# Stacked weights moved to low addresses, raw w2 rows above them, stack and bias preparation moved to earlier steps

## The chip, the cores and the metric

The kernel runs on one core of one Trainium2 chip. The metric is the device time of one execution in microseconds. The core has five engines that run in parallel, each in its own program order: PE (TensorE, matmuls; PEld is its weight load), DVE (VectorE), ACT (ScalarE), POOL (GpSimd) and SP (SyncE, which here only issues DMA transfers). SBUF is the on-chip memory; a tile there has 128 partitions, and an address below is the byte offset in each partition. PSUM takes the results of matmuls, in banks.

## The reference

A linear attention block gated by a feed-forward block, S = 2048 rows, D = 576, H = 32 heads of 18, F = 4608:

```python
xn = layernorm(A_x)
q, k, v = split(xn @ A_wqkv)                 # 32 heads
pq, pk = phi(q), phi(k)                      # phi(t) = where(t > 0, t + 1, exp(t)) + 1e-6
kv, z = sum_s pk * v, sum_s pk               # state of each head
s = ((pq @ kv) / (pq @ z + 1e-6)) @ A_wo
h = gelu(xn @ B_w1 + B_b1)                   # 2048 x 4608
g = silu(h @ B_w2 + B_b2)
return A_x + s * g
```

All is float32. The kernel keeps the accuracy by splitting each operand into a high part, which is the value rounded to PE's own format (`hi`, a copy on ACT), and a low part, the remainder (`lo`, a subtraction on DVE), and multiplies high by high, high by low and low by high.

## The kernel before, in words

The attention part comes first and ends near 281 us of the span. The feed-forward part follows: 18 chunks, two halves of the rows (`half`) times nine groups of 512 hidden columns (`c`). A chunk computes the hidden values of its group for 1024 rows and adds their product with `w2` to the accumulator `macc`. Both products use a scheme with seven block products in place of eight (`UP` and `ORDER` list them), for which sums of blocks are formed beforehand.

A chunk is laid out in 28 steps, `base` to `base + 27`. Steps 0 to 13 are the up-projection: two pairs, seven block products each, of seven matmuls with 512 columns (`Up`). The first six of the seven take `w1` operands over 128 rows of the inner dimension. The seventh, `self.w.rest(i)`, takes the *stacked weights*: D = 576 is four times 128 and a rest of 64, and the rests of a product's operands are stacked into one 128-row operand. Steps 14 to 27 are the down-projection: seven block products twice, of twelve matmuls with 288 columns (`product`). After every step `at_step` emits what the table `plans` holds for it, in the order in which `add` put it there: splits, sums, loads and stores for this chunk and the next. In this part the instructions of DVE, ACT, POOL and PE keep exactly the order in which they are emitted (`in_order`); each engine does its work in that order and waits where the next piece is not ready. SP is not in that list: the framework's scheduler orders its DMA issues, mostly as emitted.

Stacked weights. The seven rests of a pair lie in two tiles (`W1.load_rest`): two in a part of the tile `low`, in the region of the normalized input (byte 74016 to 84256 of a partition), and five in `we`, from the pool `xe` at the upper end of SBUF (187360 to 192480, two buffers). Products 1 and 2 use the former, products 3 to 7 the latter. The pool `xe` also holds `mid`, five slices of 512 columns: three for the up-projection's partial sums, `mid[:, 3]` for the temporary of product 7 of the hidden operands (`HOps.S`, steps 7 and 13, read until step 15) and `mid[:, 4]` for a `w1` temporary.

Stacks. `Rest` and `Rest2` build the stacks themselves: load four raw rows, split the first three (`hi` 0, `lo` 0, `store` 0 to DRAM), form four sums in place (`sums`), split those (`hi` 1, `lo` 1, `store` 1). Four of them are made inside the feed-forward part, in the first halves' chunks c = 2, 3, 5 and 6 (`REST_CHUNK`, `plan_rest2`). They borrow tiles of the hidden operands: the raw rows `h4h`, the first group `h1h` and `h1l`, the second group `h3h` and `h3l`. The same chunk needs `h3h` at step 12 for the high part of hidden operand 2 of the second pair (`HBUF`).

Raw `w2` rows. A chunk of the first half splits its `w2` operands from a raw tile of 1152 KB (`load_w2_raw`, pool `w2rp`, one buffer, 107808 to 117024). The one for chunk 0 is loaded during the last round of the attention part, after the raw `w1` tiles of pairs 0 and 1, in the region whose order is kept on all engines.

Bias. `load_bias` loads two halves of `b2` into one row group of `macc`, in the first half from SP before chunk 0, in the second half from POOL at step 5 of chunk 9, after the finished values there have been stored to `c_dram`. `set_bias` copies them on ACT to the rest of the four accumulators of a chunk with c = 0, at steps 10, 11, 13 and 14.

The last chunk (`plain`) and the gating end the kernel.

Of the kernel before, what the change touches and what calls it, by code (L numbers as in the profile page):

```python
# [15 lines left out]
P = 128  # L16
# [29 lines left out]
def linear_attention_gated_ffn(ctx, tc, x, wqkv, wo, w1, w1e, b1, w2, b2, out):  # L46
# [820 lines left out]
    w1p = ctx.enter_context(tc.tile_pool(name="w1p", bufs=2, reuse_waits="tile"))  # L867
    w2rp = ctx.enter_context(tc.tile_pool(name="w2rp", bufs=1, reuse_waits="tile"))

    def load_w2_raw(n):  # L870
        raw = w2rp.tile([P, 2, 2, CF // 2, HD], F32, tag="w2raw", name=f"w2raw{n}")
        nc.sync.dma_start(raw.rearrange("p r n a d -> p (r n a d)"), w2[n % NC])
        return raw
# [158 lines left out]
    class W1:  # L1032
# [49 lines left out]
        def load_rest(self):  # L1082
            n = self.n % NP
            a = xe.tile([P, 5, P], F32R, tag="we", name=f"we{self.n}", bufs=2)
            b = low[:, 16 + 2 * (n % 2) :][:, :2]
            nc.sync.dma_start(b.bitcast(F32), we_dram[n // 4][:, n % 4, :2])
            nc.sync.dma_start(a.bitcast(F32), we_dram[n // 4][:, n % 4, 2:])
            self.re = a, b
# [33 lines left out]
    kept = []  # L1122
    w1t, w2_raw0 = {}, []

# [4 lines left out]
    for r in range(NPAIR + 2):  # L1129
# [63 lines left out]
        if 1 <= r < NPAIR:  # L1193
# [10 lines left out]
            if r == 7:  # L1204
                w1t[0], w1t[1] = W1(0), W1(1)
                w2_raw0.append(load_w2_raw(0))
        if r == 0:
# [36 lines left out]
    pse.close()  # L1244
    ph2.close()
    right.close()
    psum = ctx.enter_context(tc.tile_pool(name="psum", bufs=3, space=PSUM, reuse_waits="tile"))
# [10 lines left out]
    load_x_extra(0)  # L1258
    mid = xe.tile([P, 5, 512], F32, name="mid")
    w1t[0].load_rest()  # L1260
    for d, t in kept:
        nc.sync.dma_start(d, t)
# [84 lines left out]
    class Rest2(Rest):  # L1347

        def raw(self):
            return self.tile("h4h").bitcast(F32)  # L1350

# [8 lines left out]
    def plan_rest2(base, key):  # L1360
        def load():
            rests[key] = Rest2(*key)

        add(base - 4, load)
        for at, what, *args in (
            (2, "hi", 0), (3, "lo", 0), (3, "store", 0), (3, "sums", DV), (5, "hi", 1), (6, "lo", 1), (6, "store", 1),
        ):
            add(base + at, lambda what=what, args=args: getattr(rests[key], what)(*args))

    class W2:  # L1370
# [5 lines left out]
        def load_raw(self):  # L1376
            self.raw = raw = load_w2_raw(self.n) if self.n else w2_raw0[0]
            self.B = lambda r, n: raw[:, r, n]
# [285 lines left out]
    for step in range(n_chunks):  # L1664
# [4 lines left out]
        if c == 0:  # L1669
            if half:  # L1670
                add(base + 5, load_bias, nc.gpsimd)
            for at, m in zip((10, 11, 13, 14), (C11, C21, C22, C12)):
                add(base + at, set_bias, m)
# [150 lines left out]
```

## Time and profile before

| | |
|---|---|
| median of 3 runs | 1116.15 us (1115.54 to 1118.18) |
| the profiled execution | 1114.53 us, its span 1112.8 us |
| mean granted TensorE clock | 0.997 |
| PE busy | 1091.2 us, 98% of the span |
| DVE, ACT, POOL busy | 822.9, 515.6, 459.6 us |
| DMA moved | 295.02 MB, mean 265 GB/s |

How to read the rows that follow. A row of a timeline gives the start and the duration in us, the engine, the line of the kernel, the operation, what is written and what is read (out<-in), the shapes and the number of instructions merged; in brackets stands how long the engine was idle before it and what ended that. SPq marks an issue on SP's queue, whose duration is that of the issue alone. A row of the waits gives who waited for whom, the total in us, how often, and the longest. A row of a group gives busy us and mean ns after the first bar and the idle time before it after the second. A row of a window gives its bounds, its length, the busy time and number of instructions of PE, PEld, DVE, ACT and POOL, the granted clock, the DMA share and GB/s. A matmul's duration is longer than the distance between two matmuls, since they are pipelined and their ends are modelled. Numbers in names such as `w__4785` tell one `w2` operand from another.

### The profile page before, as it was taken

To read this page: it belongs to the slowest core of one execution; us is meant where nothing else is said; L and a number is where in the kernel's file an instruction comes from. 1 tells how busy PE (TensorE), PEld (TensorE's weight loads), DVE (VectorE), ACT (ScalarE), POOL (GpSimd) and SP (SyncE) were. 2 spreads that over 40 slices of the span, in tenths; PEclk is the share of its full clock that TensorE was granted. 3 is DMA by queue.
4 is the path that set the end of the run, shared out by engine and by line. 5 is a ranking of instruction groups with operands and counts; after the bars stand their busy time and mean duration, and the time that the engine had idled before them with its cause. 6 is when DMAs were issued, how large, how long until landed. Compare 5 with 4: busy or idle time off the path is not lost.

```text
span 1112.8 us, 19015 instructions
## 1 busy us (share of the span) xinstructions
PE 1091.2 (98%) x6888; PEld 1008.3 (91%) x6888; DVE 822.9 (74%) x1284; ACT 515.6 (46%) x945; POOL 459.6 (41%) x423
## 2 busy tenths in 40 slices
PE   8999999999999999999999999999999999999998
PEld 8999999999798888889888899898898998989987
DVE  6777567996698888888888888676485674764876
ACT  7776565554645544455443544524233242242342
POOL 6855534665445254453443514324234143242310
PEclk9999999999999999999999999999999999999999
DMA  5999828887988889788896979997767677767342
GB/s 196 310 292 341 301 82 261 316 336 264 369 295 309 294 275 370 238 315 296 277 370 223 326 221 350 385 339 266 247 221 226 198 237 227 230 216 227 93 149 113
DMA packets 121051, 295.02 MB, mean 265 GB/s; under 512 B 12797, under 2 KB 36605, under 8 KB 118911
## 3 DMA queue, kind: packets, MB, share of 16 engines
q1 hardware_dynamic: 115391, 282.32, 71.7%
q0 software_dynamic: 4992, 10.32, 5.4%
q8 instruction: 54, 0.88, 0.3%
q10 hardware_dynamic: 576, 1.18, 0.3%
q14 instruction: 38, 0.31, 0.1%
HBM read 180.39 MB, written 108.66 MB: 260 GB/s over the span
## 4 chain that ended last, share of the span: by engine, by line
PE 85%; DMA 5%; DVE 5%; ACT 3%; issue 2%; POOL 1%; SPq 0%; DVEq 0%; POOLq 0%; ACTq 0%
PE pm L1468 33%; PE a L1306 8%; PE zy L1306 8%; PE e L1306 8%; PE ps_s L997 5%; PE b L1306 5%; PE pl L477 5%; PE e L421 3%; PE a L421 2%; PE z L421 2%; PE pd L1583 2%; PE ps_kva L530 1%; DMA c_dram<-macc 1%; DVE h_l L1030 1%; PE b L421 1%
## 5 line engine op out<-in xcount | busy, mean ns | idle before, releaser
L1027 ACT CAST h_h<-g 128x512 fp32r<-128x512 f32 x204 | 120.1, 621 | 148.9 <-PE pm L1468 138.3
L1030 DVE TENSOR_TENSOR h_l<-g,h_h 128x512 fp32r<-128x512 f32 x204 | 168.9, 828 | 13.3 <-ACT g L1314 3.1
L1476 DVE TENSOR_TENSOR macc<-macc,pm 128x576 f32<-128x576 f32 x136 | 102.2, 751 | 39.2 <-PE pm L1468 39.1
L1306 PE MATMUL a<-xH,wa 128*128 128x512 f32 x288 | 101.0, 391 | 0.0
L1478 DVE TENSOR_TENSOR macc<-pm,macc 128x576 f32<-128x576 f32 x98 | 73.7, 756 | 20.4 <-PE pm L1468 19.2
L1314 ACT ACTIVATE g<-b,b1c 128x512 f32<-128x512 f32 x36 | 24.8, 690 | 132.2 <-DVE b L1332 132.2
L1436 POOL TENSOR_TENSOR mid<-g 128x512 f32<-128x512 f32 x34 | 46.8, 1375 | 92.1 <-ACT g L1314 92.1
L1323 ACT COPY mid<-a 128x512 f32<-128x512 f32 x36 | 21.2, 588 | 94.6 <-PE a L1306 94.6
L1306 PEld LDWEIGHTS a<-xH,wa 128*128 128x128 f32 x288 | 54.1, 188 | 11.1
L1430 POOL TENSOR_TENSOR g<-g 128x512 f32<-128x512 f32 x34 | 50.2, 1477 | 22.4 <-DVE h_l L1030 20.8
L1326 DVE TENSOR_TENSOR mid<-b,mid 128x512 f32<-128x512 f32 x36 | 24.7, 685 | 44.7 <-PE b L1306 42.7
L1433 POOL TENSOR_TENSOR g<-g 128x512 f32<-128x512 f32 x34 | 52.3, 1538 | 11.3 <-DVE h_l L1030 9.7
L1306 PE MATMUL a<-xL,wa 128*128 128x512 f32 x144 | 56.6, 393 | 0.0
L1554 POOL TENSOR_TENSOR fin1l<-fin1h,fin1l 128x288 f32<-128x288 f32 x8 | 6.5, 808 | 119.3 <-DMA fin1l<-s_dram 85.4
L1306 PE MATMUL e<-xSH,wb 128*128 128x512 f32 x144 | 50.6, 392 | 0.5 <-DVE b L1332 0.5
L1306 PE MATMUL zy<-xSH,w 128*128 128x512 f32 x144 | 50.3, 390 | 0.0
L1306 PE MATMUL e<-xSH,w 128*128 128x512 f32 x144 | 50.3, 390 | 0.0
L1306 PE MATMUL zy<-xH,w 128*128 128x512 f32 x144 | 50.3, 390 | 0.0
L1306 PE MATMUL b<-xSH,w 128*128 128x512 f32 x144 | 50.3, 390 | 0.0
L1056 POOL TENSOR_TENSOR mid<-w1raw 128x256 f32<-128x256 f32 x17 | 14.3, 839 | 85.3 <-DMA w1raw<-w 45.9
L1427 POOL TENSOR_TENSOR g<-g 128x512 f32<-128x512 f32 x34 | 47.4, 1393 | 2.7
L1314 ACT ACTIVATE g<-e,b1c 128x512 f32<-128x512 f32 x36 | 24.8, 689 | 40.5 <-DVE e L1339 40.4
(974 smaller groups left out, 3680.1 us busy)
## 6 DMA issues: line engine op xcount, KB each, us to landing
op<-w SPq DMA_DIRECT2D x72, 256.0 KB
w<-op SPq DMA_DIRECT2D x72, 256.0 KB
we<-we_dram SPq DMA_DIRECT2D x36, 320.0 KB
w2raw<-w SPq DMA_DIRECT2D x10, 1152.0 KB
op<-w2o SPq DMA_DIRECT2D x19, 576.0 KB
w1raw<-w SPq DMA_DIRECT2D x18, 512.0 KB
op_a<-wa SPq DMA_DIRECT2D x18, 512.0 KB
wa<-op_a SPq DMA_DIRECT2D x18, 512.0 KB
```

The costliest lines, as they stand in the source:

```text
L421: nc.tensor.matmul(ps, st, mv, start=first and n == 0, stop=n == len(seq) - 1, skip_group_check=True,)
L477: nc.tensor.matmul(self.ps[n], st, self.wk(hl, k, n), start=(i == 0), stop=(i == n_all - 1))
L997: nc.tensor.matmul(self.ps[h], st[:, k, :], w[:, k, h * HD : (h + 1) * HD], start=(i == 0), stop=(i == len(self.seq) - 1),)
L1027: nc.scalar.copy(pair[0], src)
L1030: eng.tensor_tensor(pair[1], src, pair[0].bitcast(F32), op=SUB)
L1306: nc.tensor.matmul(ps.rearrange("p (c j) -> p c j", c=4), st, mv, start=first and n == 0, stop=n == len(seq) - 1, skip_group_check=True,)
L1314: nc.scalar.activation(g, ps, AF.Gelu_apprx_tanh, bias=b1c[:, f : f + 1])
L1430: tt(src[6, pr], src[5, pr], A(0, 0), op=ADD)
L1433: tt(src[3, pr], src[6, pr], A(0, 1), op=SUB)
L1468: nc.tensor.matmul(ps[:, q, :HD], hs[p][st][:, cs], m[:, p, :], start=(n == 0 and i not in CHAIN), stop=(n == len(seq) - 1), skip_group_ch ...
L1476: nc.vector.tensor_tensor(dst, dst, src, op=SUB)
L1478: nc.vector.tensor_tensor(dst, src, dst, op=ADD)
```

## The change

Three things. The five stacked weights per pair move from `xe` to a pool `wl` on the low side of SBUF, in the place of `w2rp`, which is now closed after the attention part; the raw `w2` tile moves into `xe`, behind `mid`, and the one for chunk 0 is loaded after the pools of the attention part have been closed, between the stacked weights of pairs 0 and 1. The raw rows of a stack go to `mid[:, 3]` and are loaded eight steps ahead of the chunk instead of four; the first group is prepared one step sooner, and the second one or two steps sooner (its store at step 4 instead of 6). The first two bias copies go from steps 10 and 11 to step 8 in chunk 0 and to step 9 in chunk 9.

```diff
     w1p = ctx.enter_context(tc.tile_pool(name="w1p", bufs=2, reuse_waits="tile"))
-    w2rp = ctx.enter_context(tc.tile_pool(name="w2rp", bufs=1, reuse_waits="tile"))
+    w2e = ExitStack()
+    w2rp = w2e.enter_context(tc.tile_pool(name="w2rp", bufs=1, reuse_waits="tile"))

     def load_w2_raw(n):
-        raw = w2rp.tile([P, 2, 2, CF // 2, HD], F32, tag="w2raw", name=f"w2raw{n}")
+        raw = xe.tile([P, 2, 2, CF // 2, HD], F32, tag="w2raw", name=f"w2raw{n}")
...
-            a = xe.tile([P, 5, P], F32R, tag="we", name=f"we{self.n}", bufs=2)
+            a = wl.tile([P, 5, P], F32R, tag="we", name=f"we{self.n}", bufs=2)
...
             if r == 7:
                 w1t[0], w1t[1] = W1(0), W1(1)
-                w2_raw0.append(load_w2_raw(0))
...
     ph2.close()
+    w2e.close()
     right.close()
...
     mid = xe.tile([P, 5, 512], F32, name="mid")
+    wl = ctx.enter_context(tc.tile_pool(name="wl", bufs=2, reuse_waits="tile"))
     w1t[0].load_rest()
+    w2_raw0 = load_w2_raw(0)
     for d, t in kept:
         nc.sync.dma_start(d, t)
     w1t[1].load_rest()
...
         def raw(self):
-            return self.tile("h4h").bitcast(F32)
+            return mid[:, 3]
...
-        add(base - 4, load)
+        add(base - 8, load)
         for at, what, *args in (
-            (2, "hi", 0), (3, "lo", 0), (3, "store", 0), (3, "sums", DV), (5, "hi", 1), (6, "lo", 1), (6, "store", 1),
+            (1, "hi", 0), (2, "lo", 0), (2, "store", 0), (3, "sums", DV), (4, "hi", 1), (4, "lo", 1), (4, "store", 1),
         ):
...
-            for at, m in zip((10, 11, 13, 14), (C11, C21, C22, C12)):
+            for at, m in zip((9, 9, 13, 14) if half else (8, 8, 13, 14), (C11, C21, C22, C12)):
                 add(base + at, set_bias, m)
```

More of the change, by code (lines that the diff above doesn't have):

```diff
@@ L1122, in linear_attention_gated_ffn @@
     kept = []
-    w1t, w2_raw0 = {}, []
+    w1t = {}
     def den_all(r, s):
@@ L1376, in load_raw @@
         def load_raw(self):
-            self.raw = raw = load_w2_raw(self.n) if self.n else w2_raw0[0]
+            self.raw = raw = load_w2_raw(self.n) if self.n else w2_raw0
             self.B = lambda r, n: raw[:, r, n]
```

## The prediction

> **What bounds the kernel now.** I read the page's busy times first, then the start of each chunk of the feed-forward phase on the PE timeline, then the waits, and last the timelines of the engines at each place where PE loses time. PE is the bound:
>
> ```profile
> PE 1091.2 (98%) x6888; PEld 1008.3 (91%) x6888; DVE 822.9 (74%) x1284; ACT 515.6 (46%) x945; POOL 459.6 (41%) x423
> ```
>
> A chunk is 98 matmuls of 512 columns and 168 of 288 columns and should cost the same each time. On the timeline the first matmul of a chunk is the one that writes `a` from `xH,wa`; chunk 0 starts with the first row, chunk 1 with the second, and so on, but the row of chunk 8 is left out:
>
> ```profile
> 281.22 0.39 PE L1306 MATMUL a<-xH,wa 128*128 128x512 f32 x1
> ...
> 328.58 0.40 PE L1306 MATMUL a<-xH,wa 128*128 128x512 f32 x1
> ...
> 373.43 0.40 PE L1306 MATMUL a<-xH,wa 128*128 128x512 f32 x1
> ...
> 420.93 0.40 PE L1306 MATMUL a<-xH,wa 128*128 128x512 f32 x1
> ...
> 468.31 0.40 PE L1306 MATMUL a<-xH,wa 128*128 128x512 f32 x1
> ...
> 513.14 0.40 PE L1306 MATMUL a<-xH,wa 128*128 128x512 f32 x1
> ...
> 560.18 0.40 PE L1306 MATMUL a<-xH,wa 128*128 128x512 f32 x1
> ...
> 609.11 0.40 PE L1306 MATMUL a<-xH,wa 128*128 128x512 f32 x1
> ...
> 698.79 0.40 PE L1306 MATMUL a<-xH,wa 128*128 128x512 f32 x1
> ...
> 744.86 0.40 PE L1306 MATMUL a<-xH,wa 128*128 128x512 f32 x1
> ```
>
> Differences give the length of each. Chunks 1 and 4 last 44.85 and 44.83 us, and 7 and 8 together 89.68, so 44.84 is the undisturbed length. Chunk 2 lasts 47.50, chunk 3 47.38, chunk 5 47.04 and chunk 6 48.93: 2.66 + 2.54 + 2.20 + 4.09 = 11.49 us over. Chunk 0 is 2.52 over and chunk 9 is 1.23 over. These six are all that the change's schedule edits can win: 15.2 us. Chunks 2, 3, 5 and 6 are those that prepare a stack (`REST_CHUNK`), and 0 and 9 are those that spread a bias. The waits of ACT name what happens in the four:
>
> ```profile
> ACT h_h L1027 <- DMA xe_dram<-rs1Trueh3h: 2.8, 1, 2.8
> ACT h_h L1027 <- DMA we_dram<-rs3Falseh3h: 2.7, 1, 2.7
> ACT h_h L1027 <- DMA we_dram<-rs2Falseh3h: 2.4, 1, 2.4
> ACT h_h L1027 <- DMA we_dram<-rs4Falseh3h: 1.8, 1, 1.8
> ```
>
> The second group of a stack borrows the buffers `h3h` and `h3l`. The hidden operand of product 2, second pair (`hi` (2,1), step 12), needs the same buffers and waits until the store of the stack has read them. In chunk 2, on SP, ACT and PE:
>
> ```profile
> 384.83 0.93 SPq L1024 DMA_DIRECT2D op<-w__4785  x1
> ...
> 391.11 0.64 SPq L348 DMA_DIRECT2D we_dram<-rs2Falseh3h  x1
> ```
>
> ```profile
> 386.15 0.61 ACT L333 CAST rs2Falseh3h<-rs2Falseh4h 128x512 fp32r<-128x512 f32 x1
> ...
> 398.97 0.62 ACT L1027 CAST h_h<-g 128x512 fp32r<-128x512 f32 x1 [2.39 <-DMA we_dram<-rs2Falseh3h]
> ```
>
> ```profile
> 401.51 0.53 PE L1468 MATMUL pm<-w__4567,h_h 128*128 128x288 f32 x2 [1.71 <-DVE macc L1478]
> ```
>
> The store is issued at 391.11 and lets go 7.9 us later. ACT stands in its own order, DVE waits for the low half and cannot drain the product before it, and PE runs out of free banks. In chunk 6 the wait is longest, and the clock falls behind it:
>
> ```profile
> 588.00:592.00 4.00, 3.70 (x16) 3.70 (x17) 3.02 (x4) 0.20 (x1) 3.84 (x4) 0.57 0.97 303
> ```
>
> A granted clock of 0.57 over 4 us is about 1.7 us of PE time, which is why chunk 6 loses 4.09 and not 2.5. The Trainium skill ("TensorE: Matmul & The Clock Gate", section "What's actually happening") lets the clock fall only after an idle window of about 3.4 us; here PE's halt was shorter than that (4.09 - 1.7 = 2.4 us), so the trace differs and shorter waits have to be priced with the clock too.
>
> **The change part by part.** *Stacks sooner.* In SP's order the store of the second group moves from step 6 to the head of step 4, in front of that step's three operand stores, the raw `w1` load and the `w2s` load of step 5. It then follows the store of step 3 that SP finishes at 384.83 + 0.93 = 385.76. Its data are ready: the cast of 0.61 us needs only the sums of step 3 and goes ahead of ACT's other work of step 4, and a step is 44.84 / 28 = 1.60 us. So the issue moves from 391.11 to 385.8–387, 4 to 5.3 us sooner, and the buffers come free at 393.7–395 instead of 398.97. ACT wanted them 2.39 us before 398.97, at 396.6. The margin is 1.6 to 2.9 us; the other three chunks waited 1.8 to 2.8 us, less than the move. The transfers that are passed (two operand stores, a raw load for the next chunk, a sum for step 16) come about 1 us later, with ten or more steps before they are read. ACT and DVE do the same casts one or two steps earlier, which delays the read of `e` there by up to 0.7 us; DVE and ACT catch that up where the casts used to stand. The load of the raw rows goes from 4 to 8 steps ahead, into `mid[:, 3]`, free after step 15: no cost. I take 11.49 less 0.5 for a small remaining wait: **-11.0 us**; ends 0 and -11.5.
>
> *Stacked weights low.* Five of seven products in 36 pairs use `we`: 180 matmuls.
>
> ```profile
> L1306 PE MATMUL a<-low 128*128 128x512 f32 x72 | 28.0, 389 | 0.0
> ...
> L1306 PE MATMUL e<-low,we 128*128 128x512 f32 x36 | 14.3, 397 | 0.0
> ```
>
> ```profile
> L1306 PEld LDWEIGHTS a<-low 128*128 128x128 f32 x72 | 13.5, 188 | 3.0
> ...
> L1306 PEld LDWEIGHTS e<-low,we 128*128 128x128 f32 x36 | 6.8, 188 | 1.4
> ```
>
> The two products whose stacked weights already lie low take 389 ns, those with `we` 397. If that is the address, the move gives 180 x 8 ns = **-1.4 us**; if it is not, 0. I take the first, since the moving operand of both rows is in `low` and the weights' place is what differs. The Trainium skill (same page, section "LDWEIGHTS (loading the stationary operand)") gives a load time that depends on the columns alone. The two load rows agree (188 and 188), and by it this term would be 0 and the sum 1105.5; the matmul rows disagree.
>
> *Raw `w2` rows above.* The load for chunk 0 leaves the place where it followed the raw `w1` loads and comes after the pools of the last phase are closed:
>
> ```profile
> 261.33 0.42 SPq L1087 DMA_DIRECT2D we<-we_dram  x1
> ...
> 269.55 0.38 SPq L872 DMA_DIRECT2D w2raw<-w  x1
> ```
>
> ```profile
> 289.46 0.68 ACT L1027 CAST w__3750<-w2raw 128x576 fp32r<-128x576 f32 x1
> ```
>
> Its new tile covers the place where the `we` tiles were, and a load into that place was issued at 261.33, so the space is free by then; the first cast from the tile comes at 289.46, 20 us after the old issue. I take 0; ends 0 and the late case among the rivals. The later chunks' loads do not move.
>
> *Bias copies.* They are moved, not removed. In chunk 0, on ACT, DVE and PE:
>
> ```profile
> 295.50 0.68 ACT L1027 CAST w__3837<-w2raw 128x576 fp32r<-128x576 f32 x1
> ...
> 300.89 0.69 ACT L1314 ACTIVATE g<-b,b1c 128x512 f32<-128x512 f32 x1 [3.61 <-DVE b L1332]
> 301.47 0.90 ACT L1286 COPY macc<-macc 128x864 f32<-128x864 f32 x1
> ...
> 303.38 1.15 ACT L1286 COPY macc<-macc 128x1152 f32<-128x1152 f32 x1
> ```
>
> ```profile
> 296.50 1.33 DVE L1030 TENSOR_TENSOR w__3837<-w2raw,w__3837 128x576 fp32r<-128x576 f32 x1
> ...
> 300.17 0.68 DVE L1332 TENSOR_TENSOR b<-e,mid 128x512 f32<-128x512 f32 x1
> ```
>
> ```profile
> 300.91 0.50 PE L1306 MATMUL e<-xSH,wb 128*128 128x512 f32 x1 [0.30 <-DVE b L1332]
> ...
> 306.74 0.40 PE L1468 MATMUL pm<-w__3750,h_l 128*128 128x288 f32 x1 [1.11 <-DVE h_l L1030]
> ```
>
> ACT idles 3.61 us before 300.89, so the 0.90 + 1.15 = 2.05 us fit there. But at the head of step 8 they stand before the cast at 295.50. That cast then ends at 295.50 + 2.05 + 0.68 = 298.2, and its low half on DVE starts 1.7 us after 296.50. DVE's order puts the read of `e` at 300.17 behind it, so it slips to about 301.9, and PE already waits for it at 300.91. What PE saves at 306.74 and just before (most of the 2.52 us) it pays here: I take 0. In chunk 9 the bias comes by a POOL transfer:
>
> ```profile
> 708.96 0.61 POOL L1280 DMA_DIRECT2D macc<-b  x1 [6.80 <-DMA c_dram<-macc]
> ```
>
> ```profile
> macc<-b POOLq DMA_DIRECT2D x2, 144.0 KB, 6.3
> ```
>
> ```profile
> 712.41 1.14 ACT L1027 CAST h_h<-g 128x512 fp32r<-128x512 f32 x2
> ```
>
> It lands near 708.96 + 6.3 = 715.3. At step 9 the copies stand between the two casts merged in the last row, so ACT now reaches them at 713 and waits until 715.3, ends them at 717.4, and the second cast follows 4.4 us late, on DVE's way to product 1. I take +0.4 for both chunks together: **+0.4 us**; ends -3.75 (both excesses gone) and +3.2 (chunk 0 pays 1.7 and wins nothing, and the clock falls behind it for 1.5 us, as in chunk 6).
>
> The sum is -11.0 - 1.4 + 0.4 = -12.0 us. The profiled execution took 1114.53 (span 1112.8 and 1.7 around it), 1.6 less than the median 1116.15 of the runs: 1102.5 for such a profile, and **1104.1 us** for the median.
>
> **The rivals.** (1) The bias copies take both excesses away: if POOL leaves DVE alone the low half at 296.50 could shrink from 1.33 to the 0.7 that the same operation takes elsewhere and the slip is hidden. 1104.1 - 0.4 - 3.75 = 1100.0 us. Against it stands the order above. (2) The buffers come free sooner, but not soon enough: the stores pass on to a DMA queue with megabytes ahead of them, and half of each wait stays. 1104.1 + 5.7 = 1109.8. For it: the DMA share of 0.97 in the row of chunk 6; against it: SP's issue itself moves by 4 us or more. (3) Slower than before: the raw `w2` load of chunk 0 is issued late, behind the saved operand stores, and ACT, which runs in order, stops at the cast of 289.46 while PE fills its banks. Each microsecond of landing after that costs one; it decides from 289.46 + 12.0 = 301.5 on. With the 7.9 us that the store of chunk 2 took, that is an issue after 293.6, 24 us later than now. An issue at 300 would give 1104.1 + 18.4 = 1122.5. The row at 261.33 speaks against it. (4) The address does nothing: 1105.5, inside the forecast's own range.
>
> **How the numbers follow.** Forecast (1101.5 to 1107, with (4) in it) 0.62, rival (1) 0.17, (2) 0.15, (3) 0.03, anything else 0.03, of that 0.02 within 0.3%. A measurement of this kernel tells about 0.3%, 3.3 us, from no change. The range from 1099.8 to 1109.8 takes in (1) and (2). Faster: all but (3) and the rest, and I leave 0.03 of the others for stalls that reappear: 0.92; within 0.3%: 0.05; slower: 0.03.
>
> **What would show each step right or wrong.** Right: no ACT wait on a stack's store, chunks 2, 3, 5 and 6 within 0.5 us of the undisturbed length, no stretch of chunk 6 at a clock under 0.9, `we` matmuls near 389 ns and the undisturbed chunk shorter by about 80 ns, the first `w2raw` issue before 280. Chunk 0 should show PE waiting longer for the read of `e` and less for `h_l`; chunk 9 an ACT wait for the bias. Wrong: a store of `h3h` that still lands after step 12, a cast of `w__` in chunk 0 that waits for `w2raw`, or a new wait where the moved casts delay the read of `e` in the stack chunks.

## The result, and the profile after

| | before | after |
|---|---|---|
| median of the runs | 1117.16 us (1115.54 to 1118.39, 4 runs) | 1103.62 us (1102.86 to 1105.36, 4 runs) |
| the profiled execution, its span | 1114.53, 1112.8 us | 1104.28, 1102.6 us |
| mean granted clock in it | 0.997 | 0.998 |

The ratio is 0.988 with a 95% interval of 0.986 to 0.990. The forecast was 1104.1 us, the chance for faster 0.92. The time came out as forecast, the terms only in part: between the two profiles the weights brought more than twice what was taken for them, the stacks less, and the bias copies stood at more than was taken for them. These errors cancelled in part.

PE is as full as before; the busy line of the page:

```profile
PE 1087.8 (99%) x6888; PEld 1008.0 (91%) x6888; DVE 822.6 (75%) x1284; ACT 516.7 (47%) x945; POOL 457.0 (41%) x423
```

The starts of chunks 0 to 7, 9, 10, 11 and 17 on the PE timeline of the changed kernel (lines have moved by one to three; L1309 is the old L1306):

```profile
281.40 0.39 PE L1309 MATMUL a<-xH,wa 128*128 128x512 f32 x1
...
329.81 0.40 PE L1309 MATMUL a<-xH,wa 128*128 128x512 f32 x1
...
374.94 0.40 PE L1309 MATMUL a<-xH,wa 128*128 128x512 f32 x1
...
419.59 0.40 PE L1309 MATMUL a<-xH,wa 128*128 128x512 f32 x1
...
464.48 0.40 PE L1309 MATMUL a<-xH,wa 128*128 128x512 f32 x1
...
509.13 0.40 PE L1309 MATMUL a<-xH,wa 128*128 128x512 f32 x1
...
554.57 0.40 PE L1309 MATMUL a<-xH,wa 128*128 128x512 f32 x1
...
600.02 0.40 PE L1309 MATMUL a<-xH,wa 128*128 128x512 f32 x1
...
689.32 0.40 PE L1309 MATMUL a<-xH,wa 128*128 128x512 f32 x1
...
736.06 0.40 PE L1309 MATMUL a<-xH,wa 128*128 128x512 f32 x1
...
780.71 0.40 PE L1309 MATMUL a<-xH,wa 128*128 128x512 f32 x1
...
1048.59 0.40 PE L1309 MATMUL a<-xH,wa 128*128 128x512 f32 x1
```

From chunk 11 to chunk 17 are six chunks in 267.88 us: the undisturbed chunk is now 44.65 us, 0.19 less than the 44.84 of before. Over it are: chunk 0 3.76, chunk 1 0.48, chunk 2 0.00, chunk 3 0.24, chunk 5 0.79, chunk 6 0.80, chunk 9 2.09 us. So between the first and the last of these starts:

| | before | after | difference |
|---|---|---|---|
| 17 undisturbed chunks | 17 x 44.84 | 17 x 44.65 | -3.2 |
| over it, chunks 2, 3, 5 and 6 | 11.49 | 1.83 | -9.7 |
| over it, chunk 0 | 2.52 | 3.76 | +1.2 |
| over it, chunk 9 | 1.23 | 2.09 | +0.9 |
| over it, chunk 1 | 0.01 | 0.48 | +0.5 |

That makes -10.3 us; the spans differ by 10.2. The medians differ by 13.5: the profiled execution of the kernel before was faster than all four runs of its median, and what chunks 2, 3, 5 and 6 lose differs from one execution to the next (11.49 us here, 10.5 and 14.8 in two kernels below that keep the old stack preparation). The table accounts for this pair of profiles, not for the other 3 us. The groups of the lines that showed the address before now read

```profile
L1309 PE MATMUL a<-low 128*128 128x512 f32 x72 | 28.1, 390 | 0.0
...
L1309 PE MATMUL e<-low,we 128*128 128x512 f32 x36 | 14.0, 389 | 0.0
```

so the two places of the stacked weights have become alike. Among ACT's waits there is none left for the stores of the stacks that chunks 2, 3, 5 and 6 prepare. What takes their place is short, and most of it is one row of PE's waits:

```profile
PE e L1309 <- DVE b L1335: 3.0, 4, 1.9
```

This is the read of `e` (the addition that forms `b` from `e`), which the prediction named as what could come late. Its longest instance is chunk 0. On ACT, on DVE and on PE there:

```profile
295.64 1.98 ACT L1289 COPY macc<-macc 128x864 f32<-128x864 f32 x2
297.51 0.67 ACT L1028 CAST w__3843<-w2raw 128x576 fp32r<-128x576 f32 x1
```

```profile
298.22 1.25 DVE L1031 TENSOR_TENSOR w__3843<-w2raw,w__3843 128x576 fp32r<-128x576 f32 x1 [1.56 <-ACT w__3843 L1028]
...
301.76 0.68 DVE L1335 TENSOR_TENSOR b<-e,mid 128x512 f32<-128x512 f32 x1
```

```profile
302.50 0.50 PE L1309 MATMUL e<-xSH,wb 128*128 128x512 f32 x1 [1.87 <-DVE b L1335]
```

The chain is the one worked out beforehand: two copies of 1.98 us together in front of the cast, DVE idle for 1.56, the read of `e` at 301.76 (forecast "about 301.9"). And the clock falls behind the halt; the row of the window 304 to 306 us, in which the third figure from the end is the granted clock:

```profile
304.00:306.00 2.00, 2.00 (x6) 1.55 (x5) 1.04 (x2) 0.89 (x2) 2.00 (x2) 0.50 1.03 409
```

In this stretch matmuls of 512 columns begin 0.43 us apart, elsewhere 0.23. In chunk 9, ACT and POOL:

```profile
705.79 1.98 ACT L1289 COPY macc<-macc 128x864 f32<-128x864 f32 x2 [2.05 <-DMA macc<-b]
...
710.60 0.62 ACT L1028 CAST h_h<-mid 128x512 fp32r<-128x512 f32 x1 [1.74 <-POOL mid L1439]
```

```profile
708.68 0.57 POOL L1283 DMA_DIRECT2D macc<-b  x1 [8.29 <-ACT h_h L1028]
709.27 1.30 POOL L1439 TENSOR_TENSOR mid<-g 128x512 f32<-128x512 f32 x1
```

ACT does wait for the bias. The two POOL rows show something the prediction had not seen: POOL stands for 8.29 us at the issue of the second half of the bias, and the first sum of step 7 (`mid<-g`) stands behind it. The change did not bring this wait; the kernel before has it too:

```profile
717.13 0.57 POOL L1280 DMA_DIRECT2D macc<-b  x1 [7.56 <-DMA c_dram<-macc]
```

### The profile page after: what moved, and what is told of

It is laid out like the page before. It is cut to its first block, busy times and chain, and to the rows that moved or that the text cites. A ratio compares the mean times of both kernels' runs of the same rounds, so it can differ in the third digit from the quotient of the medians.

```text
span 1102.6 us, 19034 instructions
## 1 busy us (share of the span) xinstructions
PE 1087.8 (99%) x6888; PEld 1008.0 (91%) x6888; DVE 822.6 (75%) x1284; ACT 516.7 (47%) x945; POOL 457.0 (41%) x423
## 4 chain that ended last, share of the span: by engine, by line
PE 87%; DMA 4%; ACT 4%; DVE 3%; issue 2%; POOL 1%; SPq 0%; DVEq 0%; POOLq 0%; ACTq 0%
PE pm L1471 34%; PE zy L1309 9%; PE e L1309 9%; PE a L1309 8%; PE ps_s L998 5%; PE pl L477 5%; PE b L1309 4%; PE e L421 3%; PE a L421 2%; PE z L421 2%; PE pd L1586 2%; DMA op<-w 1%; PE ps_kva L530 1%; PE b L421 1%; PE ptp L965 1%
## 5 line engine op out<-in xcount | busy, mean ns | idle before, releaser
L1031 DVE TENSOR_TENSOR h_l<-g,h_h 128x512 fp32r<-128x512 f32 x204 | 164.4, 806 | 2.4 <-ACT h_h L1028 2.4
L1309 PE MATMUL a<-xH,wa 128*128 128x512 f32 x288 | 100.8, 390 | 0.0
L1439 POOL TENSOR_TENSOR mid<-g 128x512 f32<-128x512 f32 x34 | 44.1, 1297 | 89.2 <-ACT g L1317 89.2
L1309 PEld LDWEIGHTS a<-xH,wa 128*128 128x128 f32 x288 | 54.1, 188 | 10.8
L1309 PE MATMUL a<-xL,wa 128*128 128x512 f32 x144 | 56.2, 391 | 0.0
L1309 PE MATMUL e<-xSH,wb 128*128 128x512 f32 x144 | 51.5, 399 | 3.0 <-DVE b L1335 3.0
L1309 PE MATMUL zy<-xH,w 128*128 128x512 f32 x144 | 50.7, 393 | 0.0
L1309 PE MATMUL b<-xSH,w 128*128 128x512 f32 x144 | 50.3, 390 | 0.0
L1309 PE MATMUL zy<-xSH,w 128*128 128x512 f32 x144 | 50.2, 389 | 0.0
L1309 PE MATMUL e<-xSH,w 128*128 128x512 f32 x144 | 50.2, 389 | 0.0
```

The lines of the kernel that those rows point to most:

```text
L1031: eng.tensor_tensor(pair[1], src, pair[0].bitcast(F32), op=SUB)
L1309: nc.tensor.matmul(ps.rearrange("p (c j) -> p c j", c=4), st, mv, start=first and n == 0, stop=n == len(seq) - 1, skip_group_check=True,)
```

## The experiments: one part at a time

The kernel before with the stack edit alone:

```diff
-            return self.tile("h4h").bitcast(F32)
+            return mid[:, 3]
...
-        add(base - 4, load)
+        add(base - 8, load)
...
-            (2, "hi", 0), (3, "lo", 0), (3, "store", 0), (3, "sums", DV), (5, "hi", 1), (6, "lo", 1), (6, "store", 1),
+            (1, "hi", 0), (2, "lo", 0), (2, "store", 0), (3, "sums", DV), (4, "hi", 1), (4, "lo", 1), (4, "store", 1),
```

> The kernel before with the stack edit alone (raw rows in mid[:, 3], loaded eight steps ahead, second group split and stored at step 4). Theory: the stores of h3h and h3l are what chunks 2, 3, 5 and 6 lost their time to, so this edit alone brings most of the gain: the four chunks fall from 11.49 us over the undisturbed 44.84 to the 1.84 us that the changed kernel's profile still has there (0.00, 0.24, 0.79, 0.81), -9.65 us, and all other chunks stay as they are: a profile of 1114.53 - 9.65 = 1104.9 us, ratio 0.991. Rival: the remaining 0.24, 0.79 and 0.81 us come not from the stack edit but from the raw w2 rows at their new address (DVE reads them); then this kernel has none of them and takes 1103.0 us. Second rival: with the address left as it was the stores are late all the same; then over 1108.

Measured: ratio 0.989 (0.987 to 0.991), 1105.1 us. From the start of chunk 2 to that of chunk 7, five chunks with all four stacks among them:

```profile
373.97 0.40 PE L1306 MATMUL a<-xH,wa 128*128 128x512 f32 x1
...
598.29 0.40 PE L1306 MATMUL a<-xH,wa 128*128 128x512 f32 x1
```

224.32 us for 5 x 44.84 = 224.20: 0.12 us are left of 11.49. The stack edit has almost no residue of its own; the 1.83 us of the changed kernel come only when the address edit is there too. In that the first rival is right, but not in its time of 1103.0 us: in this profile chunk 0 is 3.02 over and chunk 9 1.89 (2.52 and 1.23 before), although the bias copies stand where they stood. These two chunks lose different amounts without any edit to them.

The address edit alone (the `wl` pool, raw `w2` in `xe`, its late first load):

> The kernel before with the address edit alone (five stacked weights per pair in wl at 107808, raw w2 above mid, its first load after the attention pools are closed). Theory: the address of the weights costs 18 to 19 ns for each of the ten we matmuls of a chunk (9 to the following matmul, 5 and 4 in the two matmuls after that, by the medians of the pitches before and after), 0.19 us in each of 18 chunks: the undisturbed chunk is 44.65 and the profile 1114.53 - 3.4 = 1111.1 us, ratio 0.997. Rival 1 (the prediction's term): only the pitch to the next matmul falls, 8 ns a matmul, chunk 44.76, 1113.1 us. Rival 2: the address does nothing and the 0.19 us belong to another part of the change: chunk 44.84, 1114.5 us, ratio 1.000. In all of them chunks 2, 3, 5 and 6 keep their 11.49 us.

Measured: ratio 0.998 (0.9965 to 0.9994), 1115.65 us for 1118.41. Chunks 11 and 17:

```profile
794.17 0.40 PE L1309 MATMUL a<-xH,wa 128*128 128x512 f32 x1
...
1062.05 0.40 PE L1309 MATMUL a<-xH,wa 128*128 128x512 f32 x1
```

Six chunks in 267.88 us, 44.65 each: all of the 0.19 us belongs to this edit, and the theory with 18 to 19 ns a matmul holds against the prediction's 8. Chunks 11 to 16 split no raw `w2` tile, so the edit acts on them by places alone. `mid`, `macc` and the `w2` operands also moved, by 4 KB; in h4_low below they lie where they lay before, and an undisturbed up-projection keeps its gain. All profiles with the stationary operands at these places agree on the 44.65 within 0.01 us. The span of this profile is nevertheless 1116.0 us, since chunks 2, 3, 5 and 6 are 14.8 us over in it and chunk 9 is 4.83 over. These losses differ from one execution to the next; the ratio over many of them shows a gain of 2.2 us, in an interval (0.7 to 3.9) that holds the 3.4.

The bias edit alone:

```diff
-            for at, m in zip((10, 11, 13, 14), (C11, C21, C22, C12)):
+            for at, m in zip((9, 9, 13, 14) if half else (8, 8, 13, 14), (C11, C21, C22, C12)):
```

> The kernel before with the bias edit alone (two copies at step 8 in chunk 0, at step 9 in chunk 9). Theory: it makes the kernel slower, since in chunk 0 the two copies hold up the cast of w__3837 and with it the read of e on DVE, and in chunk 9 ACT waits for the bias transfer: chunk 0 from 2.52 to 3.75 us over the undisturbed length (the last 1.5 of them by the halved clock behind a PE wait of 2.3 us), chunk 9 from 1.23 to 2.09: +2.1 us, 1116.6 us, ratio 1.002; without the halved clock in chunk 0 +0.6, ratio 1.0005. Rival: the excesses of chunks 0 and 9 in the changed kernel come from the raw w2 rows' new address and late load; then the bias edit alone removes what PE waited for at the first product and the kernel gains up to 3.75 us, ratio 0.997.

Measured: ratio 0.9994 (0.998 to 1.0008), 1117.24 us for 1118.41. Neither the theory's +2.1 us nor the rival's -3.75 lies in the interval, which reaches from -2.2 to +0.9 us; the theory's other branch, +0.6 without the halved clock, does. In this profile chunk 0 is 3.01 and chunk 9 2.39 over, 1.65 more than before. PE halts in chunk 0 as in the changed kernel, a little longer even, but here the clock stays:

```profile
303.50 0.50 PE L1306 MATMUL e<-xSH,wb 128*128 128x512 f32 x1 [2.16 <-DVE b L1332]
```

```profile
304.00:306.00 2.00, 2.00 (x11) 1.63 (x10) 1.81 (x2) 1.89 (x4) 1.88 (x2) 1.00 1.01 401
```

What sets this can be read from the traces. In all fourteen of them the stretches of lowered clock lie on a grid: each begins a whole number of steps of 3.41 us after the trace's first clock record, and each that ends before the kernel does lasts one step. What PE did in the step before tells which steps these are. In the changed kernel the whole halt falls into one step; in bias_alone the border between two steps, near 302.6, cuts it:

```profile
299.70:303.10 3.40, 1.53 (x8) 0.94 (x7) 3.40 (x5) 0.62 (x2) 2.01 (x2) 1.00 1.02 412
303.10:306.50 3.40, 3.40 (x10) 2.66 (x9) 2.44 (x4) 2.15 (x5) 2.62 (x3) 0.50 1.04 411
```

```profile
299.20:302.60 3.40, 2.14 (x10) 1.42 (x8) 3.40 (x4) 0.67 (x2) 3.32 (x4) 1.00 1.04 415
302.60:306.00 3.40, 2.50 (x11) 2.08 (x12) 3.21 (x4) 2.41 (x4) 3.24 (x3) 1.00 1.02 411
```

Take 227 ns of work for a matmul of 512 columns and 133 for one of 288, the usual distances between starts. Then the step before the fall held 37% work in the changed kernel, and the two steps of bias_alone about 59% and 69%. From the start of the feed-forward part on, the clock fell behind every step at full clock with 38% work or less (22 of them) and behind none with 42% or more (3326). Where a halt lies on this grid differs from one execution to the next, so whether it costs the clock is chance in part.

The changed kernel without its bias edit, and the changed kernel once more:

> The changed kernel with the bias copies back at steps 10 and 11. Theory: chunk 0 returns from 3.75 to 2.52 us over the undisturbed chunk and chunk 9 from 2.09 to 1.23, so this is faster than the changed kernel: 1104.28 - 2.1 = 1102.2 us in a profile, ratio to the kernel before 0.989 less 0.002 = 0.987. Rival: with the stack and address edits in place the order of the copies no longer matters for chunk 0 (its waits come from the raw w2 rows), and it takes 1104.3 less the 0.9 of chunk 9, 1103.4.

> The changed kernel itself, beside the others on one chip. Ratio 0.988 as before. If the bias edit costs 1 to 2 us, this is 1 to 2 us above all_but_bias's 0.9861, so 0.987 to 0.988; if it costs nothing, 0.986. Chunks 3, 5 and 6 show how much their waits for the read of b and e (0.24, 0.79, 0.81 us in the first profile) differ from one execution to another.

Measured: all_but_bias 0.9861 (0.984 to 0.9882), 1102.85 us; the changed kernel, among other runs of the kernel before, 0.9866 (0.9841 to 0.9892), 1100.91 us. The intervals of the two lie over each other: what the bias edit does to the time of the whole is smaller than these runs can tell. Their profiles show chunk 0 1.39 us over without it, 4.67 and 3.76 with it, with the halved clock in both of the latter. That is the widest pair: in all profiles with the copies at 10 and 11 chunk 0 is 1.39 to 3.05 over, in the three with the edit 3.01 to 4.67. Chunk 9 is 2.42 over without it and 2.09 and 2.73 with it, and 1.23 to 4.83 in the other profiles without it, so there the edit is not shown to cause any of the loss.

## The experiments: what the residues are

Chunks 5 and 6 stand at 0.2 or 0.8 us over in every kernel with both the address edit and the stack edit (changed kernel 0.79 and 0.80, a second time 0.26 and 0.81, all_but_bias 0.21 and 0.21). PE goes through an up-projection 0.18 us faster (22.44 us before, 22.26 now), and the read of `e` by DVE, which came just in time, is now late. Whether it is 0.2 or 0.8 is seen on DVE and POOL of chunk 5, first in the changed kernel:

```profile
520.09 0.99 DVE L1031 TENSOR_TENSOR w<-w1raw,w 128x256 fp32r<-128x256 f32 x1
521.00 1.29 DVE L1031 TENSOR_TENSOR w__6364<-w2s,w__6364 128x576 fp32r<-128x576 f32 x1
```

```profile
520.04 0.75 POOL L1057 TENSOR_TENSOR mid<-w1raw 128x256 f32<-128x256 f32 x1 [6.20 <-DMA w1raw<-w]
```

then in all_but_bias, whose order is the same here:

```profile
517.41 0.42 DVE L1031 TENSOR_TENSOR w<-w1raw,w 128x256 fp32r<-128x256 f32 x1
```

```profile
517.47 0.97 POOL L1057 TENSOR_TENSOR mid<-w1raw 128x256 f32<-128x256 f32 x1 [6.29 <-DMA w1raw<-w]
```

The transfer of the raw `w1` rows lets POOL go 0.05 us before DVE's subtraction in the one and 0.06 us behind its start in the other; the same subtraction takes 0.99 us or 0.42 us, and POOL's sum 0.75 or 0.97. Whoever begins second pays. The Trainium skill ("SBUF — State Buffer", section "SBUF: two separate sides") says that a VectorE instruction with two inputs in SBUF and a GpSimd instruction that reads SBUF exclude each other from a shared port pair for their whole length. These four rows agree on who waits; with an exclusion for the whole length the second would have ended some 0.13 us later than it did. In stack_alone POOL's sum started only at 520.91, behind both subtractions (0.42 and 0.75 us), and chunk 5 was 0.1 over. That the overlap sets 0.2 or 0.8 is a reading of these profiles; no run moved POOL's sums alone.

## The experiments: what the address is worth

Two kernels on the base of all_but_bias. The first swaps `macc` and the stacked weights:

```diff
+    fl = ctx.enter_context(tc.tile_pool(name="fl", bufs=1, reuse_waits="tile"))
+    macc = fl.tile([P, QH, 5, HD], F32, name="macc")
     wl = ctx.enter_context(tc.tile_pool(name="wl", bufs=2, reuse_waits="tile"))
...
-    fl = ctx.enter_context(tc.tile_pool(name="fl", bufs=1, reuse_waits="tile"))
-
     tails = {}
-    macc = fl.tile([P, QH, 5, HD], F32, name="macc")
```

> all_but_bias with macc and the wl tiles in swapped places: the five stacked weights lie at 130848 to 135968 instead of 107808 to 112928, macc starts at 107808. Everything else is as in all_but_bias. The undisturbed chunk tells what address costs: 44.65 us with the weights at 107808, 44.84 at 187360. If the cost grows with the distance from the other w1 operands (84256 to 107808), a third of the 0.19 us comes back, 44.70 to 44.72. If there is a step in address, the chunk is one of the two, 44.65 or 44.84, and the pitch of the we matmuls 227 or 236 ns.

The second moves one pair of hidden operand tiles down:

```diff
+    h4p = ctx.enter_context(tc.tile_pool(name="h4p", bufs=1, reuse_waits="tile"))
...
-            self.ops[i, pr] = hi_lo(gp, [P, 512], f"h{HBUF[i, pr]}", 1, f"h{i}{pr}_")
+            self.ops[i, pr] = hi_lo(h4p if HBUF[i, pr] == 4 else gp, [P, 512], f"h{HBUF[i, pr]}", 1, f"h{i}{pr}_")
...
```

> all_but_bias with the two tiles of hidden operand buffer 4 (first pair's operand of products 7 and 5) moved from the upper end of SBUF to 112928, beside the stacked weights. They are the stationary side of 24 of the 168 matmuls of a down-projection. Theory S (a switch costs): a change of the stationary operand between the low and the high region and back costs the 18.6 ns seen for a we matmul; here 8 groups of three matmuls stand between others that read high tiles: 0.15 us, undisturbed chunk 44.80 us, and in products 7 and 5 the pitch rises from 133 ns at the switches. Theory H (a high address costs, every time): 24 matmuls get cheaper by up to 18.6 ns: 44.2 us. Theory N (only matmuls of 512 columns feel it): 44.65 us.

Each of the two, and the next one, ran once; what is read from them is the undisturbed chunk. Chunks 11 and 17 of the first, then of the second:

```profile
779.53 0.40 PE L1308 MATMUL a<-xH,wa 128*128 128x512 f32 x1
...
1047.41 0.40 PE L1308 MATMUL a<-xH,wa 128*128 128x512 f32 x1
```

```profile
780.24 0.40 PE L1310 MATMUL a<-xH,wa 128*128 128x512 f32 x1
...
1047.72 0.40 PE L1310 MATMUL a<-xH,wa 128*128 128x512 f32 x1
```

267.88 and 267.48 us: 44.65 and 44.58 a chunk. Between 107808 and 135968 the place makes no difference; between there and 187360 lies whatever does. In the second kernel matmuls that load from a low place stand among ones that load from a high place and the chunk got shorter by 65 ns, so in the down-projection it is not the switching that costs (theory S said +150 ns). No run tests that for the `we` matmuls, which were high ones among low ones. The sign is that of theory H, the size is not: 2.7 ns for each matmul moved, not 18.6. The next kernel moves all of them:

```diff
-    fl = ctx.enter_context(tc.tile_pool(name="fl", bufs=1, reuse_waits="tile"))
+    fl = ctx.enter_context(tc.tile_pool(name="fl", bufs=1, side="right", reuse_waits="tile"))
...
+    hp = ctx.enter_context(tc.tile_pool(name="hp", bufs=1, reuse_waits="tile"))
...
-            self.ops[i, pr] = hi_lo(gp, [P, 512], f"h{HBUF[i, pr]}", 1, f"h{i}{pr}_")
+            self.ops[i, pr] = hi_lo(hp, [P, 512], f"h{HBUF[i, pr]}", 1, f"h{i}{pr}_")
...
```

> all_but_bias with all ten tiles of the hidden operands at 112928 to 133408 and macc in their stead at the upper side: then no stationary operand of the chunks is at a high address. h_low's 24 moved matmuls brought 65 ns a chunk (44.58 for 44.65), 2.7 ns each. Theory H (each load from a high address costs): 168 matmuls, 0.45 us: undisturbed chunk 44.2 us, pitch in the down-projection about 130.5 ns, and some 8 us in 17 chunks. Theory M (what counts is that loads of both regions alternate; a run of loads from one region has the same pitch in either): the down-projection keeps its 133 ns, chunk 44.65 or a few ns from it; for this speaks that matmuls of low weights take 227 ns for 512 columns and those of high ones 133 for 288, both some 13 to 14 ns over 0.4167 ns a column. Theory A (macc is now read and written at a high address by DVE): chunk over 44.65.

```profile
781.63 0.39 PE L1310 MATMUL a<-xH,wa 128*128 128x512 f32 x1
...
1048.35 0.39 PE L1310 MATMUL a<-xH,wa 128*128 128x512 f32 x1
```

266.72 us, 44.45 a chunk: 0.20 us less than 44.65, spread over the 168 matmuls 1.2 ns each. The chunk's gain lies between theory M (none) and theory H (0.45 us). The 24 matmuls of h4_low brought 2.7 ns each and the other 144 then 0.9, so a fixed price for each matmul does not fit. In this kernel `macc` and the `w2` operands, which the down-projection streams past the hidden operands, moved up by some 20 KB; that the gain comes from the hidden operands' place alone is not shown. What `macc` costs at its new place is less than the gain. Yet this kernel took 1103.91 us, 3.1 more than the profiled all_but_bias, for its first chunk began at 286.89 us and not at 281.44. Two rows of SP's waits there:

```profile
SPq L1039 <- DMA op<-w2o: 8.2, 2, 6.7
SPq L873 <- POOL scr L935: 4.3, 1, 4.3
```

The raw `w2` tile had come to lie over a tile that POOL reads until 266 us, SP works in order, and behind that load stood three stores and then the raw `w1` load that the first chunk needs, which waits until two of the stores have landed. This is the late load of the prediction's third rival, in another kernel and by another way: not the transfer was late but what waited behind its issue.

## The experiments: towards a faster kernel

In chunk 9 the second half of the bias is issued later, behind the sums of step 8, and the copies are back at 10 and 11; in chunk 0 the copies go to the end of step 9, where ACT idles:

```diff
-                add(base + 5, load_bias, nc.gpsimd)
+                add(base + 5, load_bias, nc.gpsimd, (0,))
...
+            if c == 0 and half:
+                add(base + 8, load_bias, nc.gpsimd, (1,))
+            elif c == 0:
+                add(base + 9, set_bias, C11)
+                add(base + 9, set_bias, C21)
```

> The changed kernel with another bias edit: in chunk 0 the first two copies at the end of step 9, behind the cast of hidden operand 2 (ACT idles 3.26 us there); in chunk 9 they are back at steps 10 and 11, and the transfer of the second bias half is issued by POOL behind the sums of step 8 and not at step 5. The profile of all_but_bias has 1.39 us over the undisturbed chunk in chunk 0 and 2.42 in chunk 9. Theory: in chunk 0 PE waits at the first product because ACT does the copies between a gelu and the casts; in the idle time they cost nothing, and 0.4 us are left (the 0.33 of the up-projection). In chunk 9 POOL stands at the issue of the second half until the store of the finished values has landed (8.5 us), behind it stands the first sum of step 7, and behind that ACT's cast of it: with the sums ahead of the issue the excess falls to 0.5 us or less. Together -2.9 us: 1099.9 us for the median, ratio 0.9835. Rival 1: chunk 9 waits for ACT and DVE alone, the sum of step 7 is not on the way: its excess stays near 2.4 and only chunk 0 gains, 1101.8, ratio 0.985. Rival 2: in chunk 0 the gelu behind the copies comes late and PE waits for its bank: 1102.8 or more.

Measured: 0.9856 (0.9831 to 0.988), 1100.57 us beside 1100.91 for the changed kernel on the same chip: no difference that can be told. POOL did what the theory said:

```profile
700.09 1.29 POOL L1441 TENSOR_TENSOR mid<-g 128x512 f32<-128x512 f32 x1 [2.18 <-ACT g L1319]
...
706.70 0.59 POOL L1285 DMA_DIRECT2D macc<-b  x1 [3.95 <-DVE h_l L1031]
```

The sum of step 7 starts 2.8 us behind the first issue and not 9.5 as in the changed kernel, and the loss at the first product of chunk 9 falls from 2.04 us in all_but_bias to 0.98. But the chunk is still 1.88 over, because 0.90 is lost in its up-projection, where the seventh matmul of `a` (`a<-low`) waits for the transfer of the stacked inputs of the new half (`low<-xe_dram`); in the other profiles the up-projection of chunk 9 loses between 0 and 1.1 us. In chunk 0 the wait at the first product is gone, and the same time is lost earlier, at the read of `e` (1.15 us): DVE stood behind a low half of 1.78 us that takes 0.68 where POOL is idle.

So the low half in the way was moved, and with it all copies behind the up-projection:

```diff
-    PW2_FIRST = {1: 3, 2: 4, 7: 8, 3: 9}
+    PW2_FIRST = {1: 3, 2: 4, 3: 6, 7: 8}
...
-            for at, m in zip((10, 11, 13, 14), (C11, C21, C22, C12)):
+            for at, m in zip((13, 16, 14, 18), (C11, C21, C22, C12)):
```

> bias_in_the_gap with all four bias copies behind the up-projection (steps 13, 14, 16 and 18; the accumulators are first added to at steps 16, 18, 20 and 24), and in chunk 0 the split of w2 operand 3 at step 6 instead of 9, where DVE idles 1.94 us. In bias_in_the_gap chunk 0 was 1.41 over the undisturbed 44.65 (PE waits 1.53 us for the read of b, which stands on DVE behind two low halves of 1.06 and 1.25 us and an h_l of 1.78 us, while POOL works), chunk 9 1.88 (0.98 of it at the first product, behind ACT's copy of 1.15 us at step 11). Theory: ACT and DVE were the bound at the end of both up-projections; chunk 0 falls to 0.4 or less, chunk 9 to 1.0 or less (what its first matmuls wait for the swapped inputs stays): 2 us below bias_in_the_gap, ratio 0.984. Rival 1: DVE is not relieved, since POOL's sums then meet other subtractions: chunk 0 stays above 1.0. Rival 2: the copies at steps 14 to 18 delay ACT's casts there, and PE waits for an operand in the down-projection of chunks 0 and 9, as much as is won.

The copies of C21 and C12 read their bias from C11 and C22; at steps 16 and 18 these have already had a product added, so in this kernel (and in the one below that shares it) two of the four accumulators hold a product too many. Measured: 0.9888 (0.9865 to 0.9911), 1104.0 us. Chunk 0's up-projection is 22.24 us, not late at all, but the chunk is 3.10 over: rival 2. ACT, in order, now waits for DVE's addition into the source of each copy, and the casts behind it come late:

```profile
310.80 1.16 ACT L1291 COPY macc<-macc 128x1152 f32<-128x1152 f32 x1 [1.97 <-DVE macc L1483]
...
315.17 1.16 ACT L1291 COPY macc<-macc 128x1152 f32<-128x1152 f32 x1 [2.17 <-DVE macc L1481]
```

> no_copies_before_13 with the hidden operands low as in h_all_low. The sum of what the two bring: by theory H 8 us below no_copies_before_13 (ratio 0.977), by theory M the same time as it (0.984).

Measured: 0.9914 (0.9892 to 0.9936), 1106.9 us: the late copies' loss and the late first chunk (286.82 us) together outweigh the 0.20 us of each chunk. Neither theory is tested by its total; its undisturbed chunk is 44.45, as in h_all_low.

The last kernel takes the pieces that worked: the bias edit of bias_in_the_gap, `PW2_FIRST` as above, the hidden operands low, and the raw `w2` tile in a pool of its own under `mid`:

```diff
-        raw = xe.tile([P, 2, 2, CF // 2, HD], F32, tag="w2raw", name=f"w2raw{n}")
+        raw = wr.tile([P, 2, 2, CF // 2, HD], F32, tag="w2raw", name=f"w2raw{n}")
...
     mid = xe.tile([P, 5, 512], F32, name="mid")
+    wr = ctx.enter_context(tc.tile_pool(name="wr", bufs=1, side="right", reuse_waits="tile"))
...
```

> bias_in_the_gap (its bias copies, so all four biases are whole) with the hidden operands low and macc high as in h_all_low, but with the raw w2 tile at 193504 to 202720 and mid above it, and with the split of w2 operand 3 of chunk 0 at step 6 as in no_copies_before_13. h_all_low had an undisturbed chunk of 44.45 us for 44.65, yet its first chunk began at 286.9 us for 281.4: SP stood 4.3 us at the raw w2 load for POOL's last use of a tile that lay where that load now writes, and the raw w1 load behind it waited on. Theory: with the raw w2 tile where only tiles freed by 261 us lay, SP goes through, the first chunk begins at 281 again, and the 0.20 us of 17 chunks are won: 3.4 us below bias_in_the_gap's 1100.57, and 1.2 more in chunk 0 (its up-projection 22.24 in place of 23.68 as in no_copies_before_13, with the copies in ACT's idle time): 1096.0 us, ratio 0.9815. Rival 1: the late start has another cause (mid or macc in the place of attention tiles): first chunk at 286 to 287, 1101.4 us. Rival 2: chunk 0 gives back in the down-projection what it wins in the up-projection: 1097.2 us.

Measured: **0.981 (0.9785 to 0.9837), 1096.89 us** (1095.99 to 1097.38), faster than the kernel before and, by the narrow gap between the intervals, than the changed one, whose two intervals begin at 0.9841 and 0.9862. The issue on SP and the first chunk:

```profile
261.67 0.43 SPq L873 DMA_DIRECT2D w2raw<-w  x1
```

```profile
281.75 0.39 PE L1313 MATMUL a<-xH,wa 128*128 128x512 f32 x1
```

The load goes out 4.3 us sooner than in h_all_low and the first chunk starts 5.1 us sooner. Chunk 0 takes 44.81 us, 0.36 over, the least of all kernels here; the undisturbed chunk is 44.45. The time lies nearer to the second rival's 1097.2 than to the theory's 1096.0, but by another way: chunk 0's up-projection came out at 22.59 us and not at 22.24, and its down-projection gave nothing back.

## Why the prediction was right, point by point

- *Stacks sooner* (-11.0 taken). The mechanism was right: no wait for a store remains, no stretch of chunk 6 is slow. Alone the edit takes 11.37 of the 11.49 us away. In the company of the address edit 1.83 come back in this execution (0.74 in all_but_bias, 2.13 in the changed kernel's second profile), so in the changed kernel it brought 9.7. The residual of 0.5 us was the term mis-sized: the prediction let DVE "catch up" the earlier casts, but the read of `e` had no slack left once the matmuls ahead of it became shorter. It had named this wait among the signs of an error.
- *Stacked weights low* (-1.4 taken). The direction was right and the size was not: -3.4 us for 18 chunks, 0.19 us each. The step that failed is "180 x 8 ns". The duration of a matmul's row, 397 against 389 ns, shows only its own part. The distances between starts, worked out as medians over the 18 chunks, show the rest: behind a `we` matmul it fell from 236 to 227 ns, and in the next product behind the first three matmuls from 228, 232 and 231 to 227. That is 9 + 1 + 5 + 4 = 19 ns, ten times in a chunk. By the load time that the Trainium skill gives ("TensorE: Matmul & The Clock Gate", section "LDWEIGHTS (loading the stationary operand)"), which goes by columns alone, it would have been 0; the load rows agree with it before and after, at 188 ns, and the pace of the matmuls does not.
- *Raw `w2` rows above* (0 taken). Right: the load went out at 261.5 us, 8 us sooner than before, and no cast of chunk 0 waited. The new tile has 9216 bytes and the `we` tiles had 5120, so the row at 261.33 spoke for part of its place only; the rest was free too. What was not considered is that it now stands ahead of the raw `w1` loads on SP; that costs nothing here and cost 5 us in h_all_low.
- *Bias copies* (+0.4 taken, ends -3.75 and +3.2). In the profile +2.1: chunk 0 +1.2, chunk 9 +0.9. For chunk 0 the prediction set what is paid at the read of `e` equal to what is saved at the first product. That held roughly: PE lost 1.6 us more at the read and saved the 2.0 us at that product. What was left over is the halved clock, some 1.6 us, which had been put into the upper end only. For chunk 9 the ACT wait came as said (2.05 us), but with the copies back the chunk lost as much in other executions; POOL's wait at the second issue is a likely cause, since the loss at the first product fell where that wait was removed, but the kernel before had the same wait and lost 1.2 us there, so its share is not shown. Over many runs the edit alone does between -2.2 and +0.9 us; the +2.1 of one pair of profiles is more than that and in part chance.
- The sum. In the profile -9.7 - 3.2 + 2.1 + 0.5 = -10.3, the forecast -12.0; the medians, 1116.15 as shown first and 1103.62, differ by 12.5. The weights' surplus and the stacks' and the bias's deficit have opposite signs. That the forecast met the median within 0.5 us owes something to this. It owes as much to the runs compared: the forecast was set against 1116.15 from three runs, while the four runs of the comparison had 1117.16, and the medians of other sets of runs of the kernel before lie between 1114.63 and 1118.41.
- The rivals. (1), both excesses gone, did not come: chunk 0 is longer. (2), half of each store wait, did not come. (3) did not come in this kernel. (4), no effect of address, is refuted by address_alone. Two sums of this part were slightly off, and nothing hangs on them: with half of the 11.49 us left, rival (2) comes to 1109.4 by the forecast's own terms, not 1109.8, and the chances for faster add up to 0.91.

## What to carry to other kernels

A repeated stretch of work has one undisturbed length; take it from the starts of the stretch, and split every change into "that length" and "what is over it in which stretch". The small term multiplied by the number of stretches may be the larger one, and it must be measured by the distance between starts, not by the duration of a row. When PE becomes faster, look for the wait that had no slack: a gain on PE turned into a wait on DVE here, and a free place in one engine's order is only free if the engine that shares its port, or the queue behind it, is idle too. Before a tile is moved, ask which earlier tile lies there and what stands behind its first load on an in-order queue.

## What the runs showed of the hardware

- PE's pace depends on where in SBUF its stationary operand lies, although the load's own duration does not: 19 ns for each matmul of 512 columns whose weights lay at 187360 among weights below 107808; 1.2 ns on average for each of 288 columns when all hidden operands moved from above 192480 to below 133408 (and the operands they meet moved up). The place of the change (between 135968 and 187360 for the first) and its cause stay open.
- The clock can halve behind a halt of PE as short as 1.87 us, and can stay behind one of 2.16 us at the same place. In these traces it falls for one step of a fixed grid of 3.41 us when PE had 38% of work or less in the step before, and stays when it had 42% or more. The Trainium skill ("TensorE: Matmul & The Clock Gate", section "What's actually happening") has the clock fall after an idle window of about 3.4 us. The length agrees; the steps before the falls within the chunks were not idle but held 10 to 37% work.
- A subtraction on DVE with both inputs in SBUF took 0.42 us alone and 0.99 when a POOL sum had begun 0.05 us before it; one of 576 columns took 0.75 alone and 1.29 beside POOL. Which engine starts first by some hundredths of a microsecond was set by when a transfer landed. That this makes chunks 5 and 6 last 0.2 or 0.8 us too long is read from two profiles and not tested by a run.
